# A hand-listed order replaced by another: inducing-point attention and a SwiGLU feed-forward block on one core

## The chip, the core and the metric

The kernel runs on one core of a Trainium2 chip. Its five engines each work through a queue of their own: TensorE (PE in the profile, with its weight loads shown apart as PEld), VectorE (DVE), ScalarE (ACT), GpSimd (POOL) and SyncE (SP), which here only starts DMA transfers. The metric is the device time of one execution in microseconds (us).

## What is computed

Four batches of 12416 rows with 128 channels pass through an attention block and then, row by row, through a SwiGLU feed-forward block with 1536 hidden features. All inputs and outputs are float32.

```python
def mab(q, kv):
    s = scale * (q @ kv.transpose(0, 2, 1))
    s = s - s.max(-1, keepdims=True)
    a = np.exp(s)
    a /= a.sum(-1, keepdims=True) + 1e-09
    return a @ kv
h = mab(I, x)          # 32 inducing rows look at all rows of a batch
x = mab(x, h)          # every row looks at the 32 results
rms = np.sqrt(np.mean(x * x, axis=-1, keepdims=True) + 1e-06)
xn = x / rms * rms_g
g = xn @ w_gate
silu = g * (1.0 / (1.0 + np.exp(-g)))
val = xn @ w_val
out = silu * val @ w_out
```

## The kernel before

The second attention product and the first two feed-forward products are folded: for each batch the 32 attention results are multiplied into `w_gate` and `w_val` beforehand (the stacks `sg` and `sv`), so that a row's 32 attention weights, split into a high and a low part and laid out on 128 partitions (`a`), give gate and value directly. The rows are cut into 25 units for each of 4 batches, most of 512 rows, some of 480 or 256. The 1536 hidden features are 12 groups of 128. One unit with one group is a *block*; there are 1200 blocks, and each goes through these steps:

- `gate` (line 656) and `value` (684) on TensorE, one matmul each in the one-pass type float32r, into two PSUM banks;
- `silu` (666) on ScalarE, and `times_value` (698) on VectorE, which multiplies the two;
- then the product with `w_out`, in one of three ways, the block's *kind*.

Kind **P**: `times_value` writes to SBUF, and `project_plain` (754, the lines with `wo` in the profile) multiplies in plain float32; the profile shows two records and two weight loads for it. Kind **S**: `times_value` writes back to the value's bank; `high` (711) on ScalarE and `low` (717) on VectorE split the product into two float32r parts; `project_two` (742 and 743) multiplies both on TensorE; `add_in_place` (762) on GpSimd adds them, and `project_third` (also 754) multiplies the sum. Kind **D** is split by `high` (708) and `high_down` (730) on ScalarE with `low_of_u` (724) on GpSimd between them, and then goes on as S does. So S and D need three one-pass matmuls and P one plain one; S needs one VectorE step more than P, D one GpSimd step more than S.

```python
    for name in "".join(program.split()):
        if name == ".":
            step, args = micros[int(next(taken))]
            step(*args)
        else:
            do[name]()
```

A unit leaves through `scale_up` (786), `finish` (795), `turn_out` (801) and `store` (814). Beside the blocks run 1132 smaller steps of the attention of the following batches (loads, 32x32 transposes, scores on line 318, squares on 527, row sums on 370).

Nothing schedules at run time, and no scheduler orders the program. Up to the first gate product the order is a list of names. Everything behind it is written out in strings, searched ahead of time: `program` holds one letter for each step (g gate, s SiLU, v value, m product, h high, l low, q project_two, d add_in_place, r project_third, p project_plain, a dot for an attention step that `taken` names); `sorts` holds the kind of each block; `banks` the PSUM bank (0 to 7) that each matmul group writes; `holders` which of 19 SBUF tiles a product or part goes to; `picks` which of the waiting blocks a step takes; `workers` and `outputs` the tiles of the rest. Each engine runs its instructions in the order of that list, and semaphores make it wait for the others' results and for tiles and banks to come free. A matmul is two instructions in TensorE's queue, the weight load and the matmul; in the built program the wait stands on the pair's first one, the weight load.

Of the kernel before, what the change touches and what calls it, by code (L numbers as in the profile page):

```python
# [23 lines left out]
def kernel(  # L24
# [12 lines left out]
    m = inducing.shape[0]  # L37
# [1087 lines left out]
    def seams():  # L1125
# [16 lines left out]
        0234567120374516023741053614753614753641734617543671543613565436125461234512351364127153421432415304251034521342  # L1142
        1546243612631246347631475236423426407234673427637542374532052315034150432015245371453741037637167351675062701231
        7517017374534130142042301270432174126436741562174327156714506134614561056035462013663276261651762307157643054603
        1405364051342605341643625672174251670517614057427645705460760370274261462347347634627475617543206750135401657154
        7014605726415240657465364025423743043045012751350537056175017136731653725702170516751745246754275271263417345325
        0123102431042106524623603240546037426340731037610371057615763516370535610357413713527412534127302503243410145125
        6154572450125062012576173563057037143603607360246327407207320734263121450214352142451320461204321323131435714357
        1437513265615063105607157105612703106302610427640736273073042562364235463253462536712467126512613025710270175012
        7524317157050375136753675021706730267216471601707310434065314015341207534203524054736423450475425432501432605302  # L1150
        5430653654703570367046502305623072567506706427015460754067046274342350473543521727403430724323023607245032706547
        3476451473514354603710375073451230175017450742741765024175641327561432764126701452040674517453172651621140716472
        1046245204314212654205670251704510470274257347320545364510631643156043516045613401642063064732634732630124317461
# [12 lines left out]
        250647356270536257
    """
    workers = """
        2102102121021021020210120201010101021021021021212120201200202202020210210210210201201201212120120120120120120120
        120  # L1170
# [5 lines left out]
        abcdefghicdafjklmgnohbecfpqrslmnahjkidgboelpnqfchmrglsfnobahgpcejfhgeqlnkmbhgsripqojldenagmkhisblfrcpgohedibsjdn  # L1176
        laqmfbrkgpiceabfonlrgpqhicmsekodnjlgfimrepsqnhcbedlikgoahcbmjkprliemqbfdohsrnckgpeamjnqibkcfsldoghpmrjfkesldhain
        obkfgrcsilpmjgqenrokbgscqfmhdailjnpqrmseldohjfncbiaqkmgeprslaejobimsgdqlnpfhjarcdomekqnbjgeraodmkepjclqirsmnpkfa
        oehlrqmsjniogldscpbrkojlhqfaepsnrgmokdblipcaesqgjnhmbpflhrosqckapjefrldiongmscpqdmrefkblgaojdhpasefonqmcjrlkhgsf
        ibqmodehbclnjpkrqiasgcflmakrjeasobhpqgkjcndlifgbhasncokjgerlapmiqodscjfbkrpagqnjishblmpoqknjregadilfmspcqhgbonfk  # L1180
        liqjhmpsrofklcnqgoehjmabisdgfrkphcnjqalomgbreihcpsflbnjdaqohrkipsmngdiljeafmprcgqnksobefdgmhpraeloigfjqknbdchmps
        lfeokrbamhnicjdpoagrqeinjcskagbmleprodfgenqijpchfbgomnicrjaldesgbqpohledbfankdrmsljcgqoeabprhignqeksmpdrjlcgahfk
        obsndmpriehgaqdkjlfosrnmbliqpfgcdfikrdlomsjqapnikerfbljophgcdaikrbnmqhoifcpkandbosmprqeglainkfjehobcmprgfnqlsmho
        irafjpnkmcldsoemfbgnlqkihjgmcebradipnjmqlshfkrdcepboqagsjfhdalkcomnpfirhgbeqsjacfbcnlijqekoacrspmhbgdfkpaichrbok
        mnslegfjhdaqpmofskeircdljmgaqhbnsafklepmoqrinksoajlfpqrnmdcbghieksrofamjhcipnrgdobaqleprmhnodjkgfapceniabsjdmkqo
        lrnbephcgmifkdqplenoamrfschljgqbkimedafhrnsgmfqchbpdeljromnhkqbfpaiscgbmrneiklqdfsoghcijqsbkglphcinmajocfrsdejha
        lpiocdkbeqngrsoedkimlfjbpghadcqnrohkemisldfgpchbjqkahminsfelrbghdkjonasmfbglqpockrndaefjihglkbcpasrhneodqmlfghjn
        bqipkaomcflsgeahdjfrolcbqnmigefjsrahdgpojqklmghfdrncpseokbmjidaehrqfcgbidmaojkrhpneqfslcgekbpimnshqlocrdaspqfjkm
        hagebosmerajdqinhfckmlpojbfsrngcdqlkeimhnpacogbfimqsdhbkfronjplragmcheqgisbarkdmnojfqchigplersmaqdcnpgojhflrksqb
        gimnhfpqalcdmborjkgspnaoheigjmqrfbeloscpindehakjmsgpncbidfmkgsqjreloapihcfmbkjdegflrpahsonkcdimleqpshjonbcrgekns  # L1190
        dqmaflbriphcgjekonsladfpcbqjrgldbpeankfsqicobfrpalminsehgcodbirqgjlcfmkeongprcdajbilfmqhsopnegihrmldqcafkpjnshgo
        qekrbisacgomjpfqlngshdbfjeiqconalksgjpqdebrohalcqfimkedjnslirhdqpcjomkansriqbmgfelhdpjakqmcfraldkonqipsmhgkelcbf
        gipjrmdlnahqibkgpcleosajdbfrqlpjmahrikodgcjselnprbagckjdflqionmpsrhgebidkjcsonrlfdmghaqbkpiesocnkdjplrimqcfehasb
        ojgniclamrqdhpnksmfrlbohjkcmqspeiabfgordlnjcmhegdialbnsjqkmfdhpicoegjrhcfglhnoapgkqesjmlarcdfebpkrsigncdbmlqpofj
        naehrkbmqdljpocaerbmishlegfpnoqmdjkslcrahoipgjebqchforsipnjafmbgqdlekohcgfsrjqlihdekmopabsjcrdlnaoecigkmsocjqprk
        fljhbmpqcskgqhomlarsnq
    """
    sorts = """
        PPPPPPPPDPDPPSPPPPPPSSSSDSPSPSSPDSDPPPPDPDPPDSSSPDDSSPDSPSDSSSDPDPPPDPSDPSPPSDSPPDDSPPSPDSSDSSSSSDSPSDSSDSSSPSSS
        SDDPSSPSSPSPSPSDSSSPSSSSSSPSDPSSSDSSSDSSPSSSSSSPDSSSSPSSDSPSSSPSSPPSSSSDSSSSSSSSSSSDSPSSDSDSSSSDPSSSSDSPPSSPPSSD  # L1200
        SSPSSPDSSPSPSSSPSDPPPSDSSSPSSPSSSDDPPSPSSPDPDSSPPSSPSPSPSSSPSSSPSSSSSDSDSSSSPSDSPSSSDDPSSSPSPDSSDSPPSPSPPSSDDSPP
        SPPPDDDSDSPDSPSSPDSSSPDSPDSSPSSPDPDPDPDPSDSSSPDPSPSDSPPSPDSSDSDSPSSDPSSSDSPSDSPPDPPDSSSSSSSSSSSSPPPPSSDSPSSDSSDS
        PSSPDSSSSDSDSSSDSPPSPSSPSSSSSSDSSSPSDPSSSSSPSSPSSSDSDSSSPSDSDSPDSPPPDSDPPSSSSSSPSPSDSSSSPSSSSPSSSPSDSPPSPSDSSSSD
        PSSSPPDDSPPDSSSPSPSPSSSPSPSSPSPPSSDSSSDSSPSSSPSDDDSSPPSSSSDPSPSSSPSDPPSDPSDSDPPPSDSSDPDPDSPSPSPSPDSDSSDSDSPPPDSD
        PPSPPSDSDPSSPDSPSSDSPSDSDPPSSDPSSDSSSSSPSDSPDSPSSSPSPPSSPSSPSSSSDDPPPDSSSSDSSSSSPDSSSSDSSSSSPSSSPSDPDSSSSPSPSSSS
        SSSSSDSSSPSSPDSSSSDSSSDPSPSSPPSSSPSPSDSPDSSPSPSSDPSSSDSSPSSPPSDSSSSSPPSSPDSPSDSPPPPDSSSSSSPSPPSPSSDSSPSPSSPSDSSS
        SSSSSSPSSDSDPPPSDSSPDSDPSSPSSSPSSDPSSDSPPSSPSSSSSSSPSPSSPDSSDSSSPSPSSDSSSSSSSPSSPPSSPSPSSPDSSSSSSDSPSPSSSSPSDSSS
        PDSPSDPDSSPSPSPSSSSSSPSSPSSSSSSSDSSSPPSSSDSDSSSSPSSPSDSPDPSSPSPSSPSSSSSPSSDSSPDSSPSSSPSSSSSDPSSDSPPSSPSDSSSPPSSP
        SSPSDSSSPSSPSDSSPSSSSPDSSSSSPDSSPSSDPSSDPSSPPPSPSSPSDPPSPDSSSPPSSSPSSSSSSSPSSSSS
    """  # L1210
    picks = """
# [239 lines left out]
```

## Time and profile before

| | |
|---|---|
| median of 3 runs | 1502.98 us (1502.92 to 1503.18) |
| the profiled execution's own time | 1502.65 us |
| its span in the profile | 1500.9 us |
| granted TensorE clock | 1.0 |
| instructions in the span | 25969 |
| HBM read, written | 53.95 MB, 27.00 MB |

The span runs from the first to the last profiled instruction; what lies outside it is 1.75 us in this execution. Busy time of an engine counts its instructions' durations. On TensorE a matmul's duration is modelled and overlaps the next one's, so there the distance from one start to the next says more than the duration. "PEld" is the weight loads, which mostly run beside matmuls.

### The profile page before, as it was taken

The page shows a single profiled execution, that of the slowest core. Times are in us where ns is not written, and L with a number is a line of the kernel's source. Part 1 is how long each engine was busy: PE and PEld are TensorE (multiplying, and loading weights), DVE is VectorE, ACT ScalarE, POOL GpSimd, SP SyncE. Part 2 cuts the span into 40 slices and gives each one's busy share as a digit, 9 for nine tenths or more (in the row PEclk, how much of TensorE's full clock was granted, in tenths as well). Part 3 has the DMA queues.
Part 4 walks back from the last instruction along what each step waited for, and adds up shares of the span by engine and source line. Part 5 has one row for each costly group of instructions (what it writes and reads, how often), then busy time and mean ns, then how long its engine had stood idle before and what let it go on. Part 6 is the DMA issues. An engine that isn't in the chain of part 4 may idle for free.

```text
span 1500.9 us, 25969 instructions
## 1 busy us (share of the span) xinstructions
PE 1487.7 (99%) x7197; PEld 1101.3 (73%) x7197; DVE 1454.2 (97%) x2575; ACT 1325.7 (88%) x2743; POOL 1420.1 (95%) x1346
## 2 busy tenths in 40 slices
PE   8999999999999999999999999999999999999998
PEld 6557677776776777776787677777678777777776
DVE  6999999999999999999999999999999999999998
ACT  5899899898988889888899888989899989899986
POOL 1499999999999999999999999999999999999998
PEclk9999999999999999999999999999999999999999
DMA  7475425436572213545656222264122112222222
GB/s 284 98 113 91 95 38 108 104 83 87 84 119 45 49 35 67 113 106 102 106 102 96 43 42 40 49 130 112 27 52 39 32 37 42 36 40 39 41 37 41
DMA packets 389329, 112.56 MB, mean 75 GB/s; under 512 B 365088, under 2 KB 369728, under 8 KB 386624
## 3 DMA queue, kind: packets, MB, share of 16 engines
q1 hardware_dynamic: 388592, 110.83, 38.5%
q8 instruction: 57, 0.93, 0.3%
q14 instruction: 88, 0.72, 0.2%
q10 hardware_dynamic: 592, 0.08, 0.0%
HBM read 53.95 MB, written 27.00 MB: 54 GB/s over the span
## 4 chain that ended last, share of the span: by engine, by line
PE 91%; DVE 3%; POOL 2%; ACT 2%; issue 1%; DMA 1%; SPq 0%; DVEq 0%; ACTq 0%; POOLq 0%
PE gv L754 29%; PE gv L684 16%; PE gv L656 16%; PE gv L742 12%; PE gv L743 11%; PE gv L318 3%; PE gv L527 1%; POOL u L762 1%; PE gv L370 1%; POOL xn L762 1%; DVE gv L698 1%; PE gv L855 1%; ACT silu L666 1%; DMA xn<-in_x_dram 1%; DVE xn L717 0%
## 5 line engine op out<-in xcount | busy, mean ns | idle before, releaser
L666 ACT ACTIVATE silu<-gv 128x512 f32<-128x512 f32 (+2 forms) x1193 | 681.4, 590 | 88.6 <-PE gv L656 65.4
L656 PE MATMUL gv<-a,sg 128*128 128x512 f32 (+2 forms) x1188 | 503.7, 424 | 1.2 <-ACT silu L666 0.7
L684 PE MATMUL gv<-a,sv 128*128 128x512 f32 (+2 forms) x1188 | 464.3, 413 | 0.3 <-ACT o L786 0.3
L698 DVE TENSOR_TENSOR gv<-silu,gv 128x512 f32<-128x512 f32 (+2 forms) x684 | 447.3, 668 | 8.9 <-PE gv L684 4.2
L762 POOL TENSOR_TENSOR u<-xn,u 128x512 fp32r<-128x512 f32 (+2 forms) x308 | 379.8, 1244 | 3.4 <-PE gv L743 2.3
L762 POOL TENSOR_TENSOR xn<-xn,xn 128x512 fp32r<-128x512 f32 (+2 forms) x300 | 374.2, 1257 | 5.1 <-PE gv L743 4.8
L711 ACT ACTIVATE xn<-gv 128x512 fp32r<-128x512 f32 (+2 forms) x587 | 339.3, 586 | 28.4 <-DVE gv L698 18.9
L698 DVE TENSOR_TENSOR u<-silu,gv 128x512 f32<-128x512 f32 (+1 forms) x509 | 332.8, 666 | 6.9 <-PE gv L684 2.6
L754 PE MATMUL gv<-u,wo 128*128 128x512 f32 (+2 forms) x650 | 324.5, 585 | 0.2 <-DVE u L698 0.2
L656 PEld LDWEIGHTS gv<-a,sg 128*128 128x128 f32 x1188 | 224.2, 189 | 106.3 <-issue 23.2
L684 PEld LDWEIGHTS gv<-a,sv 128*128 128x128 f32 x1188 | 223.8, 189 | 96.5 <-ACT silu L666 15.7
L717 DVE SCALAR_TENSOR_TENSOR xn<-xn,gv 128x512 fp32r<-128x512 f32 (+2 forms) x346 | 226.0, 658 | 5.2 <-ACT xn L711 2.7
L762 POOL TENSOR_TENSOR xn<-xn 128x512 fp32r<-128x512 f32 (+2 forms) x149 | 184.2, 1242 | 4.5 <-PE gv L743 3.7
L717 DVE SCALAR_TENSOR_TENSOR u<-xn,gv 128x512 fp32r<-128x512 f32 (+2 forms) x241 | 156.1, 653 | 1.8 <-ACT xn L711 0.7
L742 PE MATMUL gv<-xn,xn 128*128 128x512 f32 (+2 forms) x389 | 150.7, 388 | 0.0
L762 POOL TENSOR_TENSOR u<-u 128x512 fp32r<-128x512 f32 (+2 forms) x118 | 147.3, 1252 | 0.9 <-PE gv L743 0.7
L754 PEld LDWEIGHTS gv<-u,wo 128*128 128x128 f32 x650 | 120.7, 190 | 28.6 <-issue 11.4
L742 PE MATMUL gv<-xn,more 128*128 128x512 f32 (+2 forms) x343 | 134.9, 393 | 0.0
L724 POOL TENSOR_TENSOR xn<-u,xn 128x512 fp32r<-128x512 f32 (+2 forms) x103 | 129.9, 1263 | 4.0 <-ACT xn L708 3.6
L730 ACT ACTIVATE xn<-xn 128x512 fp32r<-128x512 f32 (+2 forms) x170 | 106.0, 627 | 5.4 <-POOL u L724 2.9
L708 ACT ACTIVATE xn<-u 128x512 fp32r<-128x512 f32 (+2 forms) x170 | 105.9, 626 | 1.6 <-DVE u L698 0.9
L754 PE MATMUL gv<-u,xn 128*128 128x512 f32 (+2 forms) x240 | 91.4, 387 | 0.0
(215 smaller groups left out, 2371.0 us busy)
## 6 DMA issues: line engine op xcount, KB each, us to landing
out_dram<-o SPq DMA_DIRECT2D x320, 64.0 KB, 2.0
xT<-in_x_dram SPq DMA_DIRECT2D x60, 256.0 KB, 5.3
xn<-in_x_dram SPq DMA_DIRECT2D x60, 256.0 KB, 5.7
a<-hi SPq DMA_DIRECT2D x156, 64.0 KB, 2.0
a<-lo SPq DMA_DIRECT2D x156, 64.0 KB, 2.0
xn<-in_x_dram SPq DMA_DIRECT2D x5, 1024.0 KB, 9.7
xn<-w SPq DMA_DIRECT2D x18, 256.0 KB, 3.9
out_dram<-o SPq DMA_DIRECT2D x64, 60.0 KB, 2.0
```

What stands on the lines that cost most here:

```text
L656: nc.tensor.matmul(g[:, 0:T], stacks[b][0][:, ts(j, P)], halves_in_turn(one["a"][:, 0:T]), start=True, stop=True)
L666: nc.scalar.activation(sl[:, 0:T], gates.pop(n)[:, 0:T], AF.Silu)
L684: nc.tensor.matmul(v[:, 0:T], stacks[b][1][:, ts(j, P)], halves_in_turn(one["a"][:, 0:T]), start=True, stop=True)
L698: nc.vector.tensor_tensor(out=to, in0=sl[:, 0:T], in1=v[:, 0:T], op=ALU.mult)
L711: nc.scalar.activation(hi, t["u"], AF.Copy, scale=-(1.0 - 2.0 ** -13) * 2.0 ** -12)
L717: nc.vector.scalar_tensor_tensor(out=t["lo"], in0=t["hi"].bitcast(F32), scalar=4096.0, in1=t["u"], op0=ALU.mult, op1=ALU.add)
L724: nc.gpsimd.tensor_tensor(out=t["lo"], in0=t["u"], in1=t["hi"].bitcast(F32), op=ALU.subtract)
L730: nc.scalar.activation(t["hi"], t["hi"].bitcast(F32), AF.Copy, scale=-(2.0 ** -12))
L742: nc.tensor.matmul(to, weight_of(0, j), halves_in_turn(t["hi"]), start=not one["q"], stop=False)
L743: nc.tensor.matmul(to, weight_of(1, j), halves_in_turn(t["lo"]), start=False, stop=last)
L754: nc.tensor.matmul(to.rearrange("p (n h) -> p h n", h=2) if step2 else to, lhsT, rhs, start=one["left"] == NJ, stop=one["left"] == 1)
L762: nc.gpsimd.tensor_tensor(out=t["lo"], in0=t["hi"].bitcast(F32), in1=t["lo"].bitcast(F32), op=ALU.add)
```

## The change

All eight strings are replaced; all code ahead of them, up to and with the first gate product's preparation, and the loop that reads them are unchanged. The numbers of lines quoted above are the same in both kernels. The rule by which the new order was searched counts the time of TensorE's weight loads. Of each string the first lines are shown here.

```diff
     banks = """
-        0234567120374516023741053614753614753641734617543671543613565436125461234512351364127153421432415304251034521342
+        0123145672347013546013745601763510671637601375601370513603751607106532760157031576021350721352173527315743217543
...
     workers = """
-        2102102121021021020210120201010101021021021021212120201200202202020210210210210201201201212120120120120120120120
-        120
+        2102102102102102011202012120202020210210210210101012012011010101010210210210210201200120101012012012012012012012
+        012
...
     sorts = """
-        PPPPPPPPDPDPPSPPPPPPSSSSDSPSPSSPDSDPPPPDPDPPDSSSPDDSSPDSPSDSSSDPDPPPDPSDPSPPSDSPPDDSPPSPDSSDSSSSSDSPSDSSDSSSPSSS
+        PPPPPPPPPPDPPSPPPPPPSSPSDSPSPSSPDSDPPPPDPDPPDSSPSDDSSPDSPSDSSSDPDPPPDSPDPSPPSDSPPDDSPPSPDSSDSSSSSDSPSDSPDPSSPSSS
...
     program = """
-        ........ggs.vvs.vgmgs.vg.m.vgsm.s.mmvg..v.g.p.s.p...s.pms.g.sm.v..gp.s...pm..gps..v.v..pm.mgps....vgv.mv.gsmg.pm
+        ...vgg..s.sgmv.v.svgp.msg...g.gv..s..m...p...ms.mv.p...g..v.p...sg.vs..v.gm.p.msv..m.gvps.msg.g..p..vmsvm.vp.m.g
...
```

Counted over the whole strings:

| steps or entries | before | after |
|---|---|---|
| blocks of kind P | 325 | 361 |
| blocks of kind S | 688 | 654 |
| blocks of kind D | 187 | 185 |
| `project_two`, `add_in_place`, `project_third` (each) | 875 | 839 |
| `low` | 688 | 654 |
| `low_of_u`, `high_down` (each) | 187 | 185 |
| gates, values, products (each) | 1200 | 1200 |
| attention steps | 1132 | 1132 |
| bank choices | 2706 | 2706 |
| choices of an SBUF tile | 2262 | 2224 |

By batch the P blocks go from 88, 82, 80, 75 to 103, 91, 87, 80. By length, the 36 blocks that are P now are 23 of 512 rows, 6 of 480 and 7 of 256.

More of the change, by code (lines that the diff above doesn't have):

```diff
@@ new lines @@
+        5730570473061370453043240710312537213752013260725105671075416471674652170125462561536215030413503207451024532156
+        0546056420654201527016701475672653417463104360746307267346370467302437462370163073657136531027637561351030456703
+        4567045372037206427634102310263204371421420145721547107405704513270531546532164234632415672154263564352365023602
+        4653042037036270340130126124360721464317604705167301753072657365176547016475106475047624107546174065130463416341
+        6036531023104023174207017301473602134063401450125432150271350421534210535645066340654726370262365257061527450274
@@ new lines @@
+        5271052350721327172031703245320432704707502725674106417627562172534753657620346503520642045210614056120516253451
+        6412457146741620567240571045743217032570120724725761024576430572143702175027645017251674502731523471204167454570
+        1475762732534657605360154617356413624124525105246016571603516057603756371560437160547052513605103601502413065146
+        3543513471365471345712657615437650476543106743670367203213062701270243612347613676712317317521345713672432472045
+        3720574302625406324302630512631562516024163243652405274065462025174612574215732503725324730250723640752265702516
@@ new lines @@
+        4751475016451260126151652301653127650136270361524634264214567154315731617230625310516052314623406520456276342563
+        7265760257410625401625615623604356143564514274623657420743207567263724765417642176425765012046103104234364135012
+        3654065634075165041574576175601764521405724371250352302570627102371263725730735741320547132073407567326460346734
+        6273640321032634063405234206374036326504357350315604156430652345602356376546327543673572043725027523072537152752
+        0432135412341235234156035415260546307620570476021762504650452042054063206430240143520152143571404015347165740654
@@ new lines @@
+        7051472561452647147537615476713075307536012356017053740253263472645764232643243516353015041654017340365367503653
+        6753670542536275347324134263542314623065104561031436173467031670372140620624705602467256025410761702142064727320
+        7452656350614531747431401541457320437570546354763054356735207320376327321672016731256703715165736451731523412653
+        7427345027426754027652142071527107231523125025705376203765260260274657467403542635436425623561241630524610461244
+        0106107217042156201601750136547307350735407236423526024516024165421306453210461302413746103625432165150134204512
@@ new lines @@
+        qehsgjbocafprqjkhinsomalpkdbgcnefiqsarlhjobmkpqagnbcsepfhmdicrjqhamlgsponkrdefqbgojcsmaplfqnkdorihbejpclsaeomqgf
+        krinjhbfpdlqineaihjofkscdrpgnmlabfdchjngropfelihkqmsarjgbnopkfdlqamnsorhciepbfdasomeinlkqrgdcfihjpmabdksqnoejrhp
+        lfmcdiobgjfaqdekhisrplmonakcbgdieqjnbplfsmadqrgokjnhplcgfbaeqsoifdmhbckajrenmgckbfapjhlorqsndikafpmrhqdespgcnlbj
+        krgamocfebdsqhnrlpjaigbmkchfiojclsqhepagbdcfmnoljifpckrqbgasojlfedpgmckshqidnhmrjpalockdgifbcqneslmhjapobcqrefkg
+        nsjdlameibhkfgchqneimkrljspocqgrhfmdkabneipojcfqlmsnrkbjhipognqdfkemaglcsjnibhrkgdbsqhmjnapfrohelgimdksprbqciajn
@@ new lines @@
+        lkoqmgfbaiohedsjmqocfplebnkorhgsaiebpmfnscoqjphdamiglrekfcghnodskjlcmfeqprhadngsbiaqokmerfshdiencjbpgslqidkmjrhp
+        oseakfmlgcnpabdqohjigsnerkapmcljqobsgfldipnehcamrqkosjlgfecibaqjkmlordpehbqngaflshbepockjmqfinrbdpgealosmciebkjf
+        nqpsdrhgabfecldrkibjgfcnahpmofqicbjlsrednkgqhpbdeomnafigdecjsepfknidelocqmjarbhgskdpielocnqfmrjsbkanhpfemgrbcjld
+        iheqnaskhojgmlprcdefasobkpjifmlrqbghaknrjfspiecgqoifhsmbrkdlgjpaqheoncbifsmrklgedjaqsmlpofcnrjhigbcaedqkpsjgfoni
+        habrqikmldcpsorqlnjecfpkdomisqhnbgafcpinedhjokrgbsmcanqplfgdiaebnhjsodpkcrfjnmisqblohcamgbsprjehkdlifanmbqoscaer
@@ new lines @@
+        nplhbkrfgipjmsnqdcfpgkjialmnhebrdoqaspkcefglsapkiojmqncerfbmgiedloqphiabkrgmjsnleafcgqimablfpkhrbqjesprgkcdlnome
+        bqrfsjkilgahnopcfkmdliabghedfnogkqpremscafjlgdmhfcpskienqgrjafpoknbmcqeahgbisrlqdjpbkeafnsghoimclrqandbgfksojhqm
+        lifekbgnhfcqprkdaegonmlhijqfgsrbphmjoceqbknfmpdqighsjarolkebfrndhmcqpoglasijbfredkqolfrhgjpamsnbeikgcofrqnadjmhb
+        eksirglnqpojhiarcmlfdkqbgoejadhrsmjdiopknlqrcsbmhflirgakednmsflcajokhergnlpajbimedsqhkrgnpfhjlimsbekadocgnhjrmio
+        pkfbacljnsemqkolijdncbgpmfqhrksoajlefbnsdqojcpghreaifbmnlkqodhjrsmnpclkdegaiqfhnosbcjipdlegrnmspajkbgdqormcplfbh
@@ new lines @@
+        SSSPSPDSSPSPSSPSSDPPPSDSSSPPSPSSSDDPPSPSSPDPDSSPPSSPSPSPSSSPSSSPPDPPSDSDSSSSPSDSPSSSDDPPSSPSPDSSDSPPSPSPPSSDDSPP
+        SPPPPDDSDSPDSPSSPDSSSPDSPDSSPSSPDPDPDPDPSDPSSPDPPSSDSPPSPDSSDSDSPSSDSPSSDSPSDPPPDPSDSSSSSSSSSSSSPPPPSSDSPSSDSSDS
+        PSPSDSSSSDSDSSSDSPPSPSSPSSSSSSPSSSPSDPSSSSSPSSPSPSDSDSSSPSDSDSPDSPPPDSDSPPSSSSSPSPSDSSSSPSSSSPSSSPSDSPPSPSDSPSPD
+        PSSSPSDDPPPDSSSPSPSPSSSSPPSSPSPPSPDSSPDSSPSPSPSDDDSSPPSSSSDPSPSSSPSDPPSDPSDSDPPPSDSSDPDPDSPSPSPSPDSDSSDSDSPPPDDS
+        PPSPPSDDSPSSPDSSSPDSPSDSDPPSSDPSSDSSSSSPSDSPDSPSSSPSPPSSPSPSSSSSDDPPPDPSSSDSSSSPSDSSSSDSSSSSPSPSPSDPDSSSPPSPSSSS
@@ L1253 @@
[L1253 to L1255 removed]
+        ABBAAACBACAAAABBAABABAAAAAAAAAAAAAAADAAABAAAAAAADABABABACABABBBBDABAAAAAABAAAABAAADAAAABAACAAABABAAABAAABACAAAAA
+        AAAABAABAAAAAABBAABAAAAAAABAABACABAAAAAAABBBAAAAACAAABBAAAAAABABACBAACAAAAACABABAAABAAAABACABAAAABAACAACAAAACCBA
@@ new lines @@
+        AAAAAAAAABAABAAAEAAAAADAAACAAAABBABAAABACABBABAACAAABAABABAAAAABABAAABAAAAAAAAAAAAABAACBAABADBCCAABBABBBABABBAAA
+        AAAAAACACAAAAAABADBAAAAABABAAAAAAABAAAAAAACCAABAABABACAAABBAACAAAABABAAABAAAAACCABAAABAAABABAAAAABAAECACAAABAAAA
+        AAAAAAABBAAABBBBAABABAABAAABAABAAAAABAAAAAAAABAABBABABAABABBAAAABABAADBABBBAAAAAACABAABAABAACAACAAAABADAABAABDCA
+        AACDAAAAAABAAAAAAACAACBAAAAABCBAAAABAAAABCBAAAAAABAAABCDACBAAAAAABAAAAAADAABACBBAAABBCAAABABAACAAAACAACBBAAAABBA
+        AAABABAAABAAACAAAAAADAAABBBBAAABAAAABCAAACCCABBACABABBAAAABAABBAAAABAAABAABAAABBAAAABAAAABABDADAAABAABBABBABABAD
@@ new lines @@
+        BABAAAAAABAAAAAAAAAACAABAAAAAAAABCCBAACAABABAAAAAAAAAABBABBABCAAAAAABBBCABCBABABAAAABABAAACAAAAAAABAABAAAABACAAA
+        ABAAAABAAABAAAAAAAABAABAAAAABAAAAAAAAADBCAABBCCAACAAAABAAAAADBBAADABAAABAAABAAAAAAAAAABAAAAAAAADAABBAEAAAABBAACC
+        AAAAAAAAAAAAABAAABBAAAAAACAABABAABAABAAAABAAAAABAABABBAAAABAABAACABBACCAAAAABACCABABABACAAAAAAAAAABCABAABAAAACAA
+        CAAAABBACBAAAAAABAAAAAAABBAAAAAAABAABABAAACAAAAABBBAAAAAABCBAAAAABCABBABAAABABABAAABABCAAABBABAABAABAAABACBBABBA
+        ABABBAABAAAAAACAADAAAAAAAAABBAAAAEAABADABABBBAAABABAAACAAAAAAABBAAABAAAABAACABAAAAABBAABBACAAABCAAABAAAABBABAABB
@@ new lines @@
+        ABAAABACAAAAABABCCAAAABAAAACABACAABAAAAAABBAAABBABACAABAAACBAAAAAAAAAAABABAAAAABAABBACCAAAAABCABAABBAAAAAAAAABBA
+        AAAAAABAAACACBAAAAAAAAAABAAABAAAABAAACAAAAAAAAAACAAAAADBABBAAAAABAAABABBCAAABAAABABAADACCABAAAAABAAACAABABBBAAAB
+        AAAAAABAACADBAAAACABBABAAABDABABAACAAAAADABBABAAAAAAACACABBABABBABBBBAABAACBBAACCBCAABAAAAACAAACABAABAAAAAAAAABA
+        AAAAAAAAACBABBBAAAABAACAABAABAAAABAAAAABAADBABABBBAABAAFAAAAAAAAAAAABABBAAAAAAAABBABCAAABAAAABABAAAAABCAAACAAABB
+        AAABCCBBAAAAAABABAAABBAABAAACAAAAACBAABAAAABACAAAABAAAAAAABBCBABACCBAABAAAAAAACAAABABABDACAAAAAABABAABAAACAAAABA
@@ new lines @@
+        ACAABCAAABBAAAAABBAAAAABAAAAAAABABAAAAAAAACBAACAAAAAAABAFACADAAACBAAAAABBAAAAAAAAABABBADABAABACCAAAAAAAABAAAAAAA
+        AAABAABAAAAAAAABBAABAAABABACAACCBBCAAABABAABABACBBAAADAABAAAAACBABABBAAADCAAAAAAAABABBAAABAABBACABAAAABABABBAAAA
+        AAABBABAAAAABABCABBAABBAABAAAAABAACAAAAAAAAAAAAAAAABAAAAAAAAAAAABBAAAABABAAAAABACCCAAABABAAAAAACAAAAAAABAAAAABAB
+        AAAAAAAAAAAAAAACAACBACAAAABAABAAAAABBAAAAAABAAABBAABAABABBABAAAAAAAAAAAABAACACABAAAABBAABABAAABBAAAAABAAAAAAABAA
+        AAAAAAAAAAACAAABBACAADACAAAADACABAAAAAAAACAAAABCABAAABBCABABABABBAABAAAAAACABAAAAABABCBBBAAABAAAAAAAAAAABBCABDBA
@@ new lines @@
+        EBAACBAABAAACAACAABBAAAAAAAAAAAAAAABBAABABABAAACAABAAAAAAAAAAAAAAAAAAAABACAAAAAAAABAACBBAABAAAAAAAAAAACBABABBAAB
+        ACAAABAAAACAAAAAAABAAAABBAAAABAAACAAAADBABAABAAAABAABBAAABAAACAADBABBBCABABAABAAABBAAABBCBAAAAAABAAAAABAAACABAAA
+        AABBAABAAAACBAABAAAAAAABAAAABABAABABAAAAAAAAAAAAABACBCABAABAABAAAABBAAABAAAABABAAABABAAABBAAAAAAAACAAAABAAABBAAB
+        AABAAACCACAAAABAABBABAAAABDABACBBBAAAAAAABBBAAAAAABAAAAAAAABAAAABAAAAAABAAAAAAAABBAABADAAABCBCCAAAABABAAABABAAAA
+        DABBAAAABBAAAABABAAAAACAAAAABABAAABABDBCACAAAABCBAAEBCAACBADAAAABAAAABBAAAAAAABBACAAABAABAACAAACAADABCAABAABAABA
@@ L1256 @@
+        BAAAAAEAAAABAAAABAAAABAAAAACACAAABABACAABAAA
     """
     program = """
[L1258 to L1261 removed]
```

328 lines of the change are left out of this document (128 added, 200 removed), and 70 rows, old and new, of the table taken.

## The prediction

> **What bounds the kernel now.** I read the busy shares first, then the same by stretches, then the timeline of TensorE, then the waits and the groups.
>
> ```profile
> PE 1487.7 (99%) x7197; PEld 1101.3 (73%) x7197; DVE 1454.2 (97%) x2575; ACT 1325.7 (88%) x2743; POOL 1420.1 (95%) x1346
> ```
>
> Three engines look full. The stretches say which are so once the opening is over (columns: stretch, its length, then busy us and instruction count of each engine, clock, DMA share, GB/s):
>
> ```profile
> core 0: us, PE busy (x) PEld busy (x) DVE busy (x) ACT busy (x) POOL busy (x), PEclk, DMA share, GB/s
> 400.00:600.00 200.00, 199.73 (x870) 147.38 (x869) 195.25 (x349) 178.91 (x376) 196.55 (x189) 1.00 0.36 63
> 600.00:800.00 200.00, 199.88 (x1064) 151.46 (x1063) 195.04 (x343) 179.65 (x383) 197.26 (x191) 1.00 0.56 106
> 1200.00:1400.00 200.00, 200.00 (x833) 154.37 (x832) 199.48 (x334) 180.68 (x364) 199.63 (x178) 1.00 0.22 39
> ```
>
> GpSimd is busy 98 to 99.8%, VectorE 97.5 to 99.7%, while the DMA share is low and the clock full. TensorE's 100% has to be taken apart, because its durations overlap:
>
> ```profile
> 702.24 0.38 PE L656 MATMUL gv<-a,sg 128*128 128x512 f32 x1
> 702.45 0.19 PEld L684 LDWEIGHTS gv<-a,sv 128*128 128x128 f32 x1 [0.24 <-DVE xn L717]
> 702.45 0.48 PE L684 MATMUL gv<-a,sv 128*128 128x512 f32 x1
> 702.77 0.38 PE L754 MATMUL gv<-u,more 128*128 128x512 f32 x1
> ...
> 703.30 0.38 PE L754 MATMUL gv<-xn,more 128*128 128x512 f32 x1
> 703.30 0.19 PEld L754 LDWEIGHTS gv<-xn,xn 128*128 128x128 f32 x1
> 703.52 0.38 PE L754 MATMUL gv<-xn,xn 128*128 128x512 f32 x1
> 703.52 0.41 PEld L754 LDWEIGHTS gv<-u,wo 128*128 128x128 f32 x2
> 703.73 1.02 PE L754 MATMUL gv<-u,wo 128*128 128x512 f32 x2
> ...
> 704.19 0.78 PE L754 MATMUL gv<-xn,xn 128*128 128x512 f32 x1
> 704.81 0.38 PE L656 MATMUL gv<-a,sg 128*128 128x512 f32 x1
> ```
>
> A one-pass matmul of 512 columns takes 0.216 us from start to start (703.30 to 703.52). Its weights are loaded beside the matmul ahead of it (703.30), so the load costs nothing. The plain product and the matmul behind it take 1.08 (703.73 to 704.81), so the plain one takes 0.85; over all of them it is 0.853. At 702.45 a weight load could not start early, since it waited for a VectorE step that ended then; the start-to-start time is 0.32 instead of 0.216. Such a *bare load* costs 0.104.
>
> I then laid the starts of all matmul records against the sum of these streams. The streams add up to 1433 us: gates and values 503 (1920 of 0.216, 384 of 0.203, 96 of 0.110), the three matmuls of S and D 548, plain products 272, attention and opening 110. To the span's 1500.9 are missing: 1.4 ahead of the first, 4.8 behind the last, 14.8 of stalls in the first 60 us and **46.4 of stalls behind them**. The 46.4 are 310 stalls over 0.06 us and some crumbs; half of the 310 lie between 0.093 and 0.115, the size of one bare load, and only 34 (10.9 us) are over 0.15. At or right behind the attention's 32-column matmuls lie 18.9 us; the other 27.6 are mostly 178 bare loads (17.0 us).
>
> ```profile
> PEld gv L656 <- ACT silu L666: 16.7, 60, 1.1
> PEld gv L684 <- ACT silu L666: 15.7, 64, 0.5
> PEld gv L754 <- POOL u L762: 5.3, 18, 0.8
> ```
>
> The wait list (total, times, longest) shows for what the loads waited: mainly for banks that ScalarE's SiLU or VectorE frees. Idle of PEld costs only where no matmul covers it.
>
> **The change, part by part.** Prices are these rows and the following (busy and mean ns):
>
> ```profile
> L762 POOL TENSOR_TENSOR xn<-xn,xn 128x512 fp32r<-128x512 f32 x248 | 317.0, 1288 | 3.9 <-PE gv L743 3.9
> L717 DVE SCALAR_TENSOR_TENSOR xn<-xn,gv 128x512 fp32r<-128x512 f32 x272 | 183.0, 677 | 3.8 <-ACT xn L711 1.6 <-POOL u L762 0.4 <-POOL xn L762 0.3
> L711 ACT ACTIVATE xn<-gv 128x512 fp32r<-128x512 f32 x459 | 273.8, 604 | 22.6 <-DVE gv L698 14.0 <-POOL u L762 2.6 <-POOL xn L762 2.0
> ```
>
> Back to back they start closer than that: GpSimd every 1.24, VectorE every 0.60, ScalarE every 0.48 (0.52 on lines 708 and 730).
>
> *TensorE's streams, on the path:* 36 blocks trade three one-pass matmuls for a plain product: 23 x (0.853 - 0.648) + 6 x (0.800 - 0.609) + 7 x (0.427 - 0.330) = 4.7 + 1.15 + 0.7 = **+6.6 us**.
>
> *GpSimd, beside it:* 36 sums less (23 x 1.24 + 6 x 1.17 + 7 x 0.69 = 40.3) and two subtractions of D (2.5): -42.8. *VectorE:* 34 steps of line 717 less: -18.3. *ScalarE:* 34 of line 711 and two blocks' 708 and 730 less: -16.7. None of these is a saving by itself; each counts only as far as it removes stalls of TensorE.
>
> By stages of 100 gates, with the starts-apart above, GpSimd's work before is 118.4, 118.3 and 118.8 us in the third, fourth and seventh stage, which took 118.5, 118.5 and 119.7; TensorE's streams there are 114.2, 116.0 and 117.1. So in such stages GpSimd sets the pace and TensorE's stalls are its slack. After the change GpSimd's work is 114.7, 113.4 and 117.4, TensorE's 114.0, 118.1 and 118.2. Summed over the twelve stages, the larger of the two falls from 1416.5 to 1406.1: **-10.4**.
>
> *The order itself, the unknown.* The order has to keep or reduce the remaining stalls. A bare load arises where an operand or bank comes free just as the matmul ahead ends; a rule that counts the load puts such steps 0.1 us later or others ahead of them. In the built programs I counted how much TensorE work stands between the step that a matmul waits for and that matmul: under 0.5 us of it in 413 of 2854 waits for ScalarE and VectorE before, in 366 of 2822 after. That is a tenth fewer tight pairs. If stalls followed those leads alone (rates by lead from this trace), only 2 us would go; if all stalls apart from the attention's went, 27.6. An order can also be worse: stretches of 100 us in this trace hold 0.9 to 5.5 us of stalls, so 14.4 of them could hold 13 to 79, which bounds the effect at 33 less and 33 more. I take **17 less** (46.4 to about 29): the stage sums are the nearest guide, and the 10.4 that they give is net of the 6.6: 10.4 + 6.6 = 17.
>
> *Loads, stores, other queues:* the counts of DMAs are equal, and where the tiles' fills stand ahead of their first reader hardly moves. SP's transfers take 2.0 to 9.7 us; TensorE waited for DMA 0.4 us on its gates. I cost this at nothing, with a few us as the price if one fill of `a` comes late in a unit. The tail behind the last gate has 4.8 us of TensorE work against 4.7; the opening is the same.
>
> Sum: 1500.9 + 6.6 - 17 = 1490.5 of span; with 1.75 outside, 1492.2 against 1502.65; the median stands 0.33 above that execution, so **1492.5**.
>
> [...]
>
> **The rivals.**
>
> *Larger gain.* VectorE and GpSimd lose 18 and 43 us, and if their near-full load is what makes most stalls, these shrink to the attention's share: 46.4 to 20, net -20, **1483**. For it: the stretches at 98% and more. Against it: between 1200 and 1400 us both are at 99.7% and TensorE stalls only 1.8 us there, so a full neighbour does not by itself stall it; and 18.9 us hang on attention matmuls, whose number stays.
>
> *Slower: the streams win.* TensorE is the longest chain, and its streams grow by 6.6. If the new order leaves as many just-in-time banks as the old one, nothing pays for that: 1502.98 + 6.6 = **1509.6**. It decides from the point where fewer than 6.6 of the 46.4 us of stalls go. For it: leads hardly longer (2 us by rates: 1507.6), the eight banks and three SiLU buffers stay, and the stretch from 1200 has nothing left to win but gets 5 more plain products in its batch (+1.0). Against it: GpSimd-bound stages exist and are relieved.
>
> [...]
>
> *No difference.* Stalls fall by 4 to 9 us, and the plain products eat it: 1500 to 1506. That the change does not do what it says is the same case: an order searched anew that is only another one of the same worth.
>
> **How the numbers follow.** About 0.2%, 3 us, is what can be told from no change. Chances: the forecast (1487 to 1500) 0.43; larger gain (below 1487) 0.20; no difference (1500 to 1506) 0.11; slower 0.26, of it 0.08 above 1511, where the new order would add stalls of its own. Faster is 0.63. The range, 1480 to 1511, leaves about 0.08 above and 0.10 below; within the forecast alone it is 1487 to 1500.
>
> **What the next profile would show.** Plain records of line 754 at 722 and streams of about 1440. GpSimd busy near 1377, VectorE near 1435, ScalarE near 1309. If I am right, fewer loads of lines 656, 684 and 742 wait for SiLU and VectorE, and stalls behind 60 us come to some 29. If the streams win, these stalls are at 40 or more with the neighbours visibly idle. I am wrong altogether if a wait for DMA, or one late attention chain, makes a gap of several us that this trace does not have.

## The result and the profile after

The changed kernel takes **1505.61 us** (median of 18 runs, 1504.90 to 1507.38) beside 1502.91 for the kernel before on the same chip: a ratio of 1.0020, interval [1.0012, 1.0027]. It is slower by 2.7 us. Forecast were 1492.5 and faster; the time lies inside the range of 1480 to 1511.

The profiled execution's span is 1503.9 us, 3.0 more than before. First the page's busy shares, then the three stretches that were shown of before, then the waits of the loads (total, times, longest):

```profile
PE 1488.0 (99%) x7161; PEld 1106.5 (74%) x7161; DVE 1439.9 (96%) x2541; ACT 1304.0 (87%) x2705; POOL 1379.9 (92%) x1308
```

```profile
core 0: us, PE busy (x) PEld busy (x) DVE busy (x) ACT busy (x) POOL busy (x), PEclk, DMA share, GB/s
400.00:600.00 200.00, 199.99 (x867) 148.33 (x865) 193.65 (x345) 177.43 (x374) 192.44 (x186) 1.00 0.38 67
600.00:800.00 200.00, 199.44 (x1054) 151.00 (x1054) 191.63 (x337) 176.25 (x376) 189.66 (x183) 1.00 0.59 107
1200.00:1400.00 200.00, 200.00 (x830) 154.41 (x829) 198.56 (x333) 178.75 (x364) 198.07 (x176) 1.00 0.21 39
```

```profile
PEld gv L656 <- ACT silu L666: 15.4, 52, 0.8
PEld gv L684 <- ACT silu L666: 12.8, 49, 0.8
...
PEld gv L656 <- ACT o L786: 5.0, 10, 2.4
```

The neighbours did become emptier: GpSimd from 1420.1 to 1379.9 us, VectorE from 1454.2 to 1439.9, ScalarE from 1325.7 to 1304.0, and in the stretch from 600 us GpSimd from 197.26 to 189.66. The two SiLU rows shrank. The third row is new in its size: a load that waited 2.4 us for line 786, `scale_up`.

Laid against the streams as in the prediction, the matmul starts give this ledger (us; the stalls are those behind 60 us):

| kernel | streams | stalls | at or behind attention matmuls | bare loads (count) | others over 0.15 (count) | crumbs (under 0.06 each) |
|---|---|---|---|---|---|---|
| before | 1433.1 | 46.4 | 18.9 | 17.0 (178) | 4.2 (14) | 6.4 |
| after | 1439.7 | 42.8 | 19.3 | 11.2 (117) | 7.8 (18) | 4.5 |

The streams grew by 6.6 and the stalls shrank by 3.6 where 17 were forecast; with 0.3 more in the opening that is +3.3, against 3.0 by the spans. Sixty-one bare loads went (-5.8) and crumbs (-1.9), which is what a rule that counts loads should bring. But the few long stalls grew by 3.6. By stages of 100 gates, the loss is all in the first one: from the first gate to the 101st before took 131.1 us, after 136.6. The first gate starts 0.8 us earlier, and everything behind the 101st is 1.6 us shorter.

The timeline between 120 and 130 us shows where (columns: start, duration, queue or engine, line, operation, and in brackets the idle time before with its releaser):

```profile
120.91 2.22 SPq L111 DMA_DIRECT2D xT<-in_x_dram  x2
...
123.22 3.53 SPq L814 DMA_DIRECT2D out_dram<-o  x4
...
128.48 0.60 ACT L786 ACTIVATE o<-gv 128x512 f32<-128x512 f32 x1 [3.34 <-DMA out_dram<-o]
...
129.13 0.30 PEld L656 LDWEIGHTS gv<-a,sg 128*128 128x128 f32 x2 [2.43 <-ACT o L786]
129.13 0.70 PE L656 MATMUL gv<-a,sg 128*128 128x512 f32 x2 [2.03 <-ACT o L786]
```

The store of the second unit (line 814, four transfers) starts at 123.22. Its data was ready long before: `turn_out` (801) of that unit ended at 110.3. It stands on SP's queue behind the fills of `a` (594) of two units and loads of channels (111). `scale_up` of the fourth unit writes to the same `o` tile and waits 3.34 us until the store has landed. The SiLUs stand behind `scale_up` on ScalarE, and the next gate's weight load is released only by `scale_up` (129.13), so TensorE stands idle for 2.03 us. What follows costs nearly as much again:

```profile
126.00:130.00 4.00, 1.97 (x9) 1.16 (x7) 1.12 (x2) 1.52 (x4) 3.43 (x3) 1.00 0.73 108
130.00:134.00 4.00, 4.00 (x11) 2.82 (x10) 3.32 (x6) 3.46 (x9) 1.49 (x2) 0.57 0.80 124
134.00:138.00 4.00, 4.00 (x18) 3.12 (x18) 3.85 (x8) 3.21 (x7) 2.85 (x3) 1.00 0.48 94
```

From 130 to 134 us the granted clock is 0.57 (the trace has it at half from 130.13 to 133.55), and 11 matmuls run where the next stretch holds 18. Before has the second unit's store right behind the first one's (eight transfers in one row), and no such wait here:

```profile
105.99 5.34 SPq L814 DMA_DIRECT2D out_dram<-o  x8
```

A wait of `scale_up` for a store need not cost that much: at 288 us of before it waits 2.42 us for one, while TensorE has matmuls left to run, and the longest idle of TensorE in the 5 us behind it is 0.66 us.

### The profile page after: what moved, and what is told of

Same layout as the page of the kernel before. It is cut to its first block, busy times and chain, and to the rows that moved or that the text cites. A ratio compares the mean times of both kernels' runs of the same rounds, so it can differ in the third digit from the quotient of the medians.

```text
span 1503.9 us, 25837 instructions
## 1 busy us (share of the span) xinstructions
PE 1488.0 (99%) x7161; PEld 1106.5 (74%) x7161; DVE 1439.9 (96%) x2541; ACT 1304.0 (87%) x2705; POOL 1379.9 (92%) x1308
## 4 chain that ended last, share of the span: by engine, by line
PE 94%; DVE 3%; DMA 1%; ACT 1%; issue 1%; SPq 1%; POOL 0%; DVEq 0%; ACTq 0%; POOLq 0%
PE gv L754 31%; PE gv L656 17%; PE gv L684 17%; PE gv L742 11%; PE gv L743 11%; PE gv L318 3%; PE gv L527 1%; PE gv L370 1%; PE gv L855 1%; DVE u L698 1%; DMA xn<-in_x_dram 1%; PE gv L154 0%; PE gv L464 0%; DMA out_dram<-o 0%; DVE we L228 0%
## 5 line engine op out<-in xcount | busy, mean ns | idle before, releaser
L656 PE MATMUL gv<-a,sg 128*128 128x512 f32 (+2 forms) x1188 | 456.4, 419 | 2.8 <-ACT o L786 2.0
L684 PE MATMUL gv<-a,sv 128*128 128x512 f32 (+2 forms) x1188 | 448.5, 417 | 1.2 <-DVE u L698 0.5
L698 DVE TENSOR_TENSOR gv<-silu,gv 128x512 f32<-128x512 f32 (+2 forms) x650 | 422.8, 669 | 10.4 <-PE gv L684 3.5
L698 DVE TENSOR_TENSOR u<-silu,gv 128x512 f32<-128x512 f32 (+2 forms) x543 | 352.5, 661 | 17.9 <-PE gv L684 7.1
L754 PE MATMUL gv<-u,wo 128*128 128x512 f32 (+2 forms) x722 | 356.6, 581 | 1.1 <-DVE u L698 1.0
L711 ACT ACTIVATE xn<-gv 128x512 fp32r<-128x512 f32 (+2 forms) x556 | 324.1, 592 | 37.7 <-DVE gv L698 30.3
L762 POOL TENSOR_TENSOR u<-xn,u 128x512 fp32r<-128x512 f32 (+2 forms) x271 | 338.3, 1259 | 15.4 <-PE gv L743 11.2
L717 DVE SCALAR_TENSOR_TENSOR xn<-xn,gv 128x512 fp32r<-128x512 f32 (+1 forms) x347 | 224.5, 657 | 4.8 <-ACT xn L711 3.4
L754 PEld LDWEIGHTS gv<-u,wo 128*128 128x128 f32 x722 | 134.5, 190 | 33.0 <-issue 14.2
L742 PE MATMUL gv<-xn,xn 128*128 128x512 f32 (+2 forms) x369 | 146.6, 397 | 0.0
L717 DVE SCALAR_TENSOR_TENSOR u<-xn,gv 128x512 fp32r<-128x512 f32 (+2 forms) x209 | 137.0, 661 | 3.1 <-ACT xn L711 2.0
L754 PE MATMUL gv<-xn,xn 128*128 128x512 f32 (+2 forms) x227 | 87.0, 393 | 0.0
```

The costliest lines, as they stand in the source:

```text
L656: nc.tensor.matmul(g[:, 0:T], stacks[b][0][:, ts(j, P)], halves_in_turn(one["a"][:, 0:T]), start=True, stop=True)
L684: nc.tensor.matmul(v[:, 0:T], stacks[b][1][:, ts(j, P)], halves_in_turn(one["a"][:, 0:T]), start=True, stop=True)
L698: nc.vector.tensor_tensor(out=to, in0=sl[:, 0:T], in1=v[:, 0:T], op=ALU.mult)
L711: nc.scalar.activation(hi, t["u"], AF.Copy, scale=-(1.0 - 2.0 ** -13) * 2.0 ** -12)
L717: nc.vector.scalar_tensor_tensor(out=t["lo"], in0=t["hi"].bitcast(F32), scalar=4096.0, in1=t["u"], op0=ALU.mult, op1=ALU.add)
L742: nc.tensor.matmul(to, weight_of(0, j), halves_in_turn(t["hi"]), start=not one["q"], stop=False)
```

## The experiments

Two theories stood at the start. *A, the store:* the new order would have been faster, and one store put late on SP's queue takes it back. *B, the streams win:* TensorE's streams decide, the neighbours' load hardly matters, and the stalls that go are the few tight pairs. Later runs ask what holds the rest. Each ratio is to the kernel before, run beside it.

### The store moved back up

In the changed order, the letter O of the second unit goes directly behind the first.

```diff
-        Oqlhrvqsldp.g..dgrsqm. ... hFg.hvlrdsgOmgpsTvsnmqh
+        OOqlhrvqsldp.g..dgrsqm. ... hFg.hvlrdsgmgpsTvsnmqh
```

> The changed kernel with one letter of its order moved: the second unit's store stands right behind the first unit's store on SP's queue, ahead of two input loads, one gather and two more loads. In the changed kernel ScalarE's line 786 waits 3.34 us at 125 us for that store, TensorE stands still for 2.2 us, and the granted clock is half for 3.4 us from 130 us on. Theory A (the change's own gain is there, 3 to 5 us of it lost to this one wait and the slow clock behind it): span shorter by 3.5 to 5.5 us, about 1501 us in time, ratio to the kernel before 0.998 to 0.9995, no stretch at half clock behind 60 us. Rival (the order is simply no better; the wait is absorbed by slack that comes later): under 1.5 us shorter, 1504 to 1506.

Measured: 1500.62 us (before 1503.24), 0.9985 [0.9976, 0.9994]: 5.0 us less than after (5.3 with each taken against the kernel before beside it). The stalls are 38.1, those over 0.15 us fell from 7.8 (18) to 3.0 (10), and the slow stretch is gone:

```profile
113.78 5.34 SPq L814 DMA_DIRECT2D out_dram<-o  x8
...
125.99 0.60 ACT L786 ACTIVATE o<-gv 128x512 f32<-128x512 f32 x1
```

```profile
126.00:130.00 4.00, 4.00 (x18) 2.98 (x17) 3.83 (x8) 3.60 (x8) 4.00 (x4) 1.00 0.86 135
130.00:134.00 4.00, 4.00 (x18) 2.98 (x17) 4.00 (x8) 3.71 (x10) 3.70 (x5) 1.00 0.95 147
```

`scale_up` starts at 125.99 with no wait, the clock stays at 1.00, and 18 matmuls run in each 4 us. Theory A holds for the sign. It doesn't hold for the size: the order freed of this wait gains 2.6 us on before, not 10.

### The same store made late in the old order

The reverse on before: the second unit's O goes behind the two units' fills and the loads, as it stands in after.

```diff
-        ... rn.vsglp.sF. ... qnm.vOv.vg.pmmqsdp.a. ... gvrh.m.dhmsq
+        ... rn.vsglp.sF. ... qnm.vv.vg.pmmqsdp.a. ... gvrh.Om.dhmsq
```

> The kernel before with one letter moved the other way: the second unit's store, which there stands with the first one's ahead of a gather, is put where the changed kernel has it, behind two gathers and three input loads. Theory A (this place of the store alone costs the changed kernel its 5 us): ScalarE's line 786 waits for the store, TensorE stands 1 to 2.5 us near 125 us, perhaps with a stretch of half clock; 2 to 6 us slower, 1505 to 1509. Rival (the wait needs the rest of the new order): within 1 us of before.

Measured: 1507.68 us (before 1503.3), 1.0032 [1.0020, 1.0045], +4.4. The old order falls into the same hole:

```profile
121.43 3.96 SPq L814 DMA_DIRECT2D out_dram<-o  x4
...
127.11 0.60 ACT L786 ACTIVATE o<-gv 128x512 f32<-128x512 f32 x1 [3.54 <-DMA out_dram<-o]
...
127.76 0.48 PE L742 MATMUL gv<-xn,more 128*128 128x512 f32 x1 [2.95 <-ACT o L786]
```

TensorE idles 2.95 us here, and the clock is at half from 128.13 to 131.54. So the place of one store costs 4.4 us in the old order and some 5 in the new one.

### The new kinds in the old order

Before, with 35 blocks turned from S to P (15, 8, 7 and 5 by batch); the plain product stands where the block's third matmul stood, and its h, l, q and d are dropped.

```diff
     sorts = """
-        PPPPPPPPDPDPPSPPPPPPSSSSDSPSPSSPDSDPPPPD
+        PPPPPPPPDPDPPSPPPPPPSPSSDPPPPSSPDSDPPPPD
```

> The kernel before, its order kept, with 35 of its S blocks turned into P (15, 8, 7, 5 by batch, as many as the change has more, less one of 256 rows): their steps high, low, project_two and add_in_place are dropped and the plain product stands where the third matmul stood. TensorE's streams grow by 6.5 us, GpSimd loses some 40, VectorE 18, ScalarE 15. If TensorE's streams are the path and the relief of the others is worth little: +3 to +7 us (1506 to 1510). If GpSimd's load sets the pace in most stages, as the prediction had it: -5 to -10 us (1493 to 1498).

Measured: 1515.94 us (before 1503.24), 1.0083 [1.0070, 1.0097], +12.7, outside both expected ranges. The streams grow by 6.5, as priced, and the stalls do not fall; they rise from 46.4 to 53.5 with 195 bare loads. Fewer steps on GpSimd and VectorE bring nothing in an order that isn't made for them. Part of the new stalls may come from the tiles: a plain product holds its tile from `times_value` on, and ahead of the `times_value` steps that write such tiles VectorE now idles 17.6 us in total, against 6.9 before. The new order without its late store does about the same kinds in 1500.62, some 15 us less. That is at most what the search of the order brings, since the plain products were placed by hand here.

### GpSimd halved

Before, with `add_in_place` on half of each block's columns; the other half of the parts goes unsummed into the third matmul. All else is as it was.

```diff
-        nc.gpsimd.tensor_tensor(out=t["lo"], in0=t["hi"].bitcast(F32), in1=t["lo"].bitcast(F32), op=ALU.add)
+        w = unit_of(*blocks[n][:2])["T"] // 2
+        nc.gpsimd.tensor_tensor(out=t["lo"][:, 0:w], in0=t["hi"].bitcast(F32)[:, 0:w], in1=t["lo"].bitcast(F32)[:, 0:w], op=ALU.add)
```

> The kernel before with GpSimd's add_in_place on half of each block's columns (the other half of the sum is left out): GpSimd loses some 500 of its 1420 us, TensorE's streams and everything else stay. If GpSimd's load set the pace in stages (prediction's step): at least 10 us faster, 1480 to 1493. If TensorE's streams and bare loads bind: 0 to 5 us faster, 1498 to 1503.

Measured: 1500.5 us (before 1503.24), 0.9981 [0.9972, 0.9989], -2.7. Its page:

```profile
PE 1485.8 (99%) x7197; PEld 1104.3 (74%) x7197; DVE 1453.3 (97%) x2575; ACT 1323.8 (88%) x2743; POOL 975.6 (65%) x1346
```

GpSimd loses 445 us of work, its share falls from 95% to 65%, and the time falls by 2.7 us. The stalls go from 46.4 to 44.7. So GpSimd alone does not set the pace of the old order, however full its stretches look.

### TensorE relieved

Before, with gate and value matmuls of 480 instead of 512 columns from block 61 on; the last 32 columns of those blocks are left as they were in the bank.

```diff
+        T = min(T, 480) if n > 60 else T
```

> The kernel before with the gate and value matmuls of the 512-row units cut to 480 columns behind block 60 (the last 32 columns keep what the bank held): about 1800 matmuls of 0.203 instead of 0.216 us, 24 us less on TensorE, all other engines' work unchanged. If TensorE's streams are the path: 14 to 24 us faster (1479 to 1489). If GpSimd or VectorE set the pace: under 8 us faster.

Measured: 1497.85 us (before 1503.24), 0.9964 [0.9951, 0.9978], -5.4. The streams fall by 24.0 to 1409.1, and the stalls rise from 46.4 to 65.9; bare loads from 178 to 316. Of the work taken from TensorE less than a quarter shows. By the expectation that points to GpSimd or VectorE. GpSimd in the stretch from 400 us:

```profile
400.00:600.00 200.00, 199.75 (x875) 147.09 (x874) 195.86 (x352) 180.04 (x379) 197.62 (x190) 1.00 0.36 63
```

It is at 98.8% here, so the next run takes GpSimd's work away as well.

### Both relieved

The two edits above together, on before.

```diff
+        T = min(T, 480) if n > 60 else T
...
+        w = unit_of(*blocks[n][:2])["T"] // 2
```

> The kernel before with both cuts at once: gates and values of 512 columns on 480 behind block 60 (TensorE -24 us) and GpSimd's add_in_place on half the columns (GpSimd about -445). Each alone gave 5.4 and 2.7 us. Theory C (TensorE and GpSimd hold each other: what one gives, the other takes): together 16 to 24 us, 1479 to 1487. Rival D (VectorE's and ScalarE's steps between them, or the order itself, hold TensorE): the sum of both or little more, 7 to 11 us, 1492 to 1496.

Measured: 1493.14 us (before 1503.07), 0.9935 [0.9920, 0.9950], -9.9, beside -8.1 for the two alone: rival D's range. With GpSimd at 65% the stalls are still 61.2, with 281 bare loads: 14 of the 24 us remain lost.

### TensorE and VectorE relieved

The short matmuls with `times_value` of S blocks on half the columns (from block 61 on), on before.

```diff
-            nc.vector.tensor_tensor(out=to, in0=sl[:, 0:T], in1=v[:, 0:T], op=ALU.mult)
+            w = T // 2 if kind == "S" and n > 60 else T
+            nc.vector.tensor_tensor(out=to[:, 0:w], in0=sl[:, 0:w], in1=v[:, 0:w], op=ALU.mult)
```

> The kernel before with the gates and values cut as above (TensorE -24 us) and VectorE's product on half the columns for the S blocks behind block 60 (VectorE about -180 us; the other half keeps the value alone). GpSimd keeps its work. Theory C: VectorE is not what takes the gain back, 5 to 8 us faster than before (1495 to 1498). Rival D: VectorE does, and 14 to 24 us come out (1479 to 1489).

Measured: 1493.44 us (before 1503.07), 0.9935 [0.9920, 0.9949], -9.6, between the two expected ranges. VectorE loses 131 us instead of 180 and is at 89%; the stalls are 60.9. VectorE relieved brings as much as GpSimd relieved, so neither of the two alone holds the rest. Both together, and ScalarE, were not relieved.

### TensorE relieved in the new order

The run with the store moved up, with the short matmuls.

```diff
-        Oqlhrvqsldp. ...
+        OOqlhrvqsldp. ...
...
+        T = min(T, 480) if n > 60 else T
```

> The changed kernel with the early store (1500.6) and the gates and values cut as above (TensorE -24 us of its 1440). GpSimd is at 92% here and not at 95%. If GpSimd's near-full load took the gain back in the old order: 12 to 24 us faster than 1500.6 (1477 to 1489), since here it has room. If an order fixed for other durations takes it back: 4 to 8 us (1492 to 1497), as in the old order.

Measured: 1495.06 us (before 1503.07), 0.9947 [0.9932, 0.9961]: 5.6 us below the same order with full matmuls. Of 24 us the new order passes on as little as the old one (5.4), although GpSimd is at 92% instead of 95%. Stalls 38.1 to 55.7, bare loads 111 to 230. What limits a saving on TensorE is therefore not the share by which GpSimd is full.

### Three loads moved up

The order with the store moved up, with one channel load of the second batch moved ahead of a row load, and two row loads of the fourth batch moved ahead of a store. Their dots in `program` move with them.

```diff
-        ... 207 594 141 595 596 125 147 597 ...
+        ... 207 594 125 141 595 596 147 597 ...
...
-        ... 484 483 539 922 540 ... 932 495 933 508
+        ... 484 483 539 507 495 922 540 ... 932 933 508
```

> The changed kernel with the early store and three loads moved ahead on SP's queue: one channel load of batch 1 ahead of the row load in front of it (TensorE stood 1.25 us at 152 us, when VectorE waited for that set's last load), and two row loads of batch 3 ahead of a store (TensorE stood 0.85 us at 988 us for them). Theory A: both stalls go, 1 to 2 us faster, 1498.5 to 1499.6. Rival: other waits take their place, 1500 to 1501.5.

Measured: 1499.73 us (before 1503.07), 0.9978 [0.9969, 0.9988], 0.9 less than without, which is between the two expected ranges and hardly more than can be told from no change. The stalls fall from 38.1 to 36.5, most of it at attention matmuls (19.7 to 18.1). The two idles are gone, but at 1434 us TensorE now idles 0.80 us behind line 786.

### A second store moved up

The run above, with the store of unit 92 ahead of the gathers of unit 96.

```diff
-        ... hgrmqsarldrhvrmhgpldslhggOqmsdvqsFge
+        ... hgrmqsOarldrhvrmhgpldslhggqmsdvqsFge
```

> The changed kernel with the early store and the three early loads, and one store more moved ahead: that of unit 92 in front of the gathers of unit 96, since line 786 waited for it at 1431 us and TensorE stood 0.96 us. Theory A: that stall goes, 0.5 to 1 us faster than 1499.7, 1498.6 to 1499.4. Rival: no change that shows, 1499.5 to 1500.5.

Measured: 1499.56 us (before 1503.3), 0.9976 [0.9968, 0.9985]. Beside the run above no difference shows, as the rival had it: the idle at 1434 us is gone, and the stalls are the same (36.4). This version is faster than both kernels, 3.7 us below before and some 6 below after.

### Still more plain blocks

The order with the store moved up, with 32 further blocks turned from S to P in the way of the new kinds in the old order.

```diff
     sorts = """
-        PPPPPPPPPPDPPSPPPPPPSSPSDSPSPSSPDS
+        PPPPPPPPPPDPPSPPPPPPSSPSDSPSPSPPDS
```

> The changed kernel with the early store (1500.6), with 32 more S blocks turned into P (14, 7, 7, 4 by batch; 23 of 512 rows, 6 of 480, 3 of 256), the plain product standing where the third matmul stood. TensorE's streams grow by 6.1 us, GpSimd loses 38, VectorE 17. If plain products are bought at the price of their streams, and an order not made for them adds stalls as it did in the old one: 6 to 13 us slower, 1507 to 1514. If the relief of the others pays (the prediction's step): 1495 to 1501.

Measured: 1514.82 us (before 1503.3), 1.0079 [1.0064, 1.0094], 14.2 above the same order without and a little more than the 13 expected at most. Its page:

```profile
PE 1497.5 (99%) x7129; PEld 1097.7 (73%) x7129; DVE 1426.3 (94%) x2509; ACT 1292.5 (85%) x2673; POOL 1345.0 (89%) x1276
```

GpSimd and VectorE fall further, to 89% and 94%, and the time rises: 6.2 us of streams and 7.0 of stalls (45.1). So further plain blocks need an order made for them too. The reverse, plain blocks of the new order turned back to S or D, was not tried.

## Why the prediction was wrong, step by step

**TensorE's streams, +6.6:** right. They are 1439.7 after 1433.1, and line 754 has its 722 plain records. The two runs that turn 35 and 32 blocks by hand confirm the price per block with 6.5 and 6.2.

**GpSimd, VectorE and ScalarE beside it:** the sizes were near. Busy times of 1379.9, 1439.9 and 1304.0 us stand against forecasts of 1377, 1435 and 1309.

**Loads, stores, other queues, at nothing:** wrong, and this decides the sign. The step looked at the fills of `a` and at counts of DMAs, not at where each store stands on SP's queue and who needs its tile next. Its "few us as the price" was the right size, attached to the wrong transfer. One store behind two units' fills and loads cost some 5 us (4.4 in the old order). The sentence "I am wrong altogether if a wait for DMA ... makes a gap of several us that this trace does not have" named the row that came. The strings show it in part: `outputs` gives the second and the fourth unit the same `o` tile, and from O of the second to E (`scale_up`) of the fourth there are 110 steps in `program` before and 33 after. That distance alone does not tell, since both orders have about as short ones at later units (from 22 steps before, from 30 after) that cost nothing of this size; it takes the transfers ahead of the store on SP's queue as well.

**The stage sums, -10.4, "GpSimd sets the pace":** wrong. In the third, fourth and seventh stage GpSimd's work nearly equals the stage's time, and I took that for a bound. But halving its sums brings 2.7 us, not the 10 that the stage sums let go. The stages themselves did not follow either: forecast by the larger of the two sums were 114.7, 118.1 and 118.2 us, and by the starts of their gates they took 117.5, 119.9 and 120.6 after 118.5, 118.5 and 119.7. In this fixed order an engine is 98% busy in such stages and still has its work done in time nearly everywhere: the sum of an engine's work says what time a stage can't go below, not what it would fall to.

**The order itself, 17 less:** the mechanism was right as far as the runs show it (fewer bare loads, though none isolates the rule), and the term was mis-sized: 3.6 us of stalls went, 8.3 with the store on time. Bare loads fell by 61 of 178, and the loads' waits for SiLU fell with them (line 656 from 16.7 to 15.4 us, line 684 from 15.7 to 12.8). Without the late store the stalls fall by 8.3 (46.4 to 38.1), and with three loads moved up by 9.9; the 17 was taken from the stage sums, which have just fallen. With 8.3 in its place and the store on time the sum would be 1500.9 + 6.6 - 8.3 = 1499.2 of span, against 1500.2 in that run's profile; the 1.0 left lies ahead of 60 us in that execution. So of the 13.4 us by which the stalls were missed (17 against 3.6), 8.7 go back to the stage sums and 4.7 to the store. That the time still lies in the range is owed to the rivals, which widened it upward, and not to the sum. My other guide, the share of leads under 0.5 us, gave only 2 and was too low.

**The rivals.** *The streams win* came nearest: its turning point, fewer than 6.6 us of stalls gone, was met with 3.6, and its sign, stalls at 40 or more, came with 42.8. That is luck as to the cause: its reason, just as many just-in-time banks, is not what happened: the bank and operand waits paid for the streams and 1.7 us more, and one store took 5 back. *The larger gain* would have needed full neighbours to make the stalls; the runs that relieve one of them at a time speak against it; GpSimd and VectorE were not relieved together. 18.9 us did hang on attention matmuls, as was argued, and 19.3 still do.

The weight loads' busy share does not tell the kernels here apart: it is 73 or 74% on the pages of before, after and seven of the runs, whether they take 1493 us (both relieved) or 1515 (more plain blocks). The bare loads, which carry a wait, do cost time: with sixty-one of them less (178 to 117), their stalls fell by 5.8 us (17.0 to 11.2).

**What stays open.** Of 24 us taken from TensorE 5.4 arrive, and about 10 when GpSimd or VectorE is relieved too. The rest comes back as bare loads (178 to 316, then 281 and 253). That a list made for one set of durations keeps each step just in time for the others, so that only a new list would collect the saving, fits all these runs, but it was argued and not shown. Two rivals stand beside it: GpSimd and VectorE may hold TensorE by turns, which only a run that relieves both would tell, and ScalarE, whose SiLUs cost the loads of gate and value the longest waits (16.7 and 15.7 us before), was never relieved. Nor is it shown what the search would reach with the 325 plain blocks of before, so how much of the 2.6 us is the order's and how much the kinds' stays open.

## What to carry to other kernels

When an order is replaced, follow every queue that it feeds: for each store ask which transfers stand ahead of it and which step needs its buffer next, above all while the first buffers go round. A neighbour's busy share, even 98%, is not a bound until a run that takes much of its work away shows the time to follow; here 445 of 1420 us less moved it by 0.2%. And a plain block is cheap only in an order that was made for it: a like exchange cost 12.7 us by hand and less than nothing with the searched order once its store was on time.

## What the hardware showed that was not expected

Two idles of TensorE cost more than their own length. Idles of 2.03 us (after) and 2.95 us (the late store in the old order) were each followed, 1.0 and 0.4 us after they ended, by 3.41 us at half the granted clock, with starts of one-pass matmuls 0.43 us apart instead of 0.216:

```profile
128.89 0.63 PE L684 MATMUL gv<-a,sv 128*128 128x512 f32 x1
129.32 0.63 PE L742 MATMUL gv<-xn,xn 128*128 128x512 f32 x1
129.75 0.63 PE L743 MATMUL gv<-u,xn 128*128 128x512 f32 x1
```

These rows are from the timeline of the late store in the old order. Half the clock for 3.41 us loses 1.7 us of work (an estimate, 0.5 x 3.41), so most of what the late store cost, 4.4 us in the old order and some 5 in the new, is the idle and the slow stretch behind it. Idles of 0.73 us (after, ended at 155.24) and 0.66 us (before, ended at 292.50) were followed by no such stretch: the granted clock is 1.00 in the 4 us behind them.
